# A causal segment's feature map with one exponential for all keys and one for all queries, in a four-layer attention kernel on one core

## The chip, the core and the metric

The kernel runs on one core of one Trainium2 chip. The metric is the device time of one execution in microseconds (us), lower is better. The core has five engines that run their own instruction queues and wait for each other by semaphores: PE (matrix products), ACT (exponentials and other functions), DVE (elementwise work, reads PSUM), POOL (elementwise work in SBUF) and SP (issues transfers).

## The reference

Four layers stand one behind the other on 2048 tokens of width 512, with 32 heads of 16 columns: causal segments with a memory (A), full attention (B), A, B. Cut to what matters:

```python
def _A_ref(x, wq, wk, wv, wo, beta):          # N = 4 segments of L = 512 tokens
    phi = lambda t: jnp.where(t > 0, t + 1.0, jnp.exp(t))
    for s in range(N):
        qs, ks, vs = (q[:, :, s].copy(), k[:, :, s].copy(), v[:, :, s].copy())
        p = _softmax(jnp.einsum('bhqd,bhkd->bhqk', qs, ks) * scale + mask, axis=-1)
        a_dot = jnp.einsum('bhqk,bhkd->bhqd', p, vs)
        pq = phi(qs)
        num = jnp.einsum('bhld,bhde->bhle', pq, M)
        den = jnp.einsum('bhld,bhd->bhl', pq, z)[..., None] + 1e-06
        outs.append(g * (num / den) + (1.0 - g) * a_dot)
        pk = phi(ks)
        M = M + jnp.einsum('bhld,bhle->bhde', pk, vs)
        z = z + jnp.einsum('bhld->bhd', pk)
    return joined(outs) @ wo

def _B_ref(x, wqkv, wo):                      # full attention over 2048 tokens
    p = _softmax(jnp.einsum('bhqd,bhkd->bhqk', q, k) * Dh ** (-0.5), axis=-1)
    return joined(jnp.einsum('bhqk,bhkd->bhqd', p, v)) @ wo

x = x + _A_ref(_layernorm(x), ...)            # and B, A, B in the same way
```

The feature map phi is applied to the queries of segments 1 to 3 and to the keys of segments 0 to 2, in two A layers: six times each.

## The kernel before

**Units.** Scores are made in banks: one PSUM bank holds 128 keys of one head against 512 queries. The main loop (attention, one turn is a *unit*) takes two or three banks; PE multiplies masked queries (qm) with keys, ACT takes one exponential over the unit's banks (L1925, ps to pT, 1024 or 1536 columns), and two units later PE multiplies values by pT. Two sets of three banks alternate, so PE can be at most two units ahead of ACT. Other banks of scores do not go to ACT: a unit of two banks leaves room for one or two *taken* banks, whose exponentials DVE makes with integer arithmetic in bf16 bits (L1394, ps to a tile of sixteen-bit integers) and two sums of it with constants (L1450 and L1493 on DVE, L1475 on POOL). PE multiplies values by the three parts. The integer tile is dxt, or KA, QA, VA, wA or wB while those are free. So a bank costs either ACT a third of a unit or DVE, POOL and PE some work each. On the causal diagonal the mask is a product with tri on PE, or a select on pT by POOL (L1939) where PE is late.

**Tasks between units.** Layer norms, projections (xT with wA or wB, evacuated from PSUM by DVE, or by ACT in a copy at L757), the memory and the output projection are generators (task_A, task_mem, task_B, task_out). Each yields its needs with its cost on PE and DVE; the loop resumes one when its needs are met and it fits.

**The order.** Every instruction is recorded ahead of time by a planner (Sched) that keeps an estimated time of each engine; the program that runs is the fixed order per engine that comes out. How eager each kind of work is (how late DVE may be, how many banks are taken, when PE is kept busy with products on zeros, who does a mask) is set by some 60 limits, chosen for every stretch of 20 units in the table PLAN; a limit that a row leaves out has its default. A new limit or a new cost anywhere changes all that is planned behind it.

**The feature map.** task_A calls phi four times per segment: for keys, after four transposes through the DMA (phk from KA), in two halves of 1024 columns; for queries in two halves from QA to phq. Each half has an exponential on ACT into the tile amem (L966), then on DVE max(x, 0) + 1 (L968) and the minimum with the exponential (L969). amem also carries the memory's output (task_mem, L1059) through a transpose into phq, so a half waits until amem is free. The memory's output is later added to oT by DVE (L1211) or POOL (L1186, L1208). The masked queries qm of the next group are made on POOL as well (L1802).

Of the kernel before, what the change touches and what calls it, by code (L numbers as in the profile page):

```python
# [6 lines left out]
ACT = mybir.ActivationFunctionType  # L7
ALU = mybir.AluOpType
# [408 lines left out]
class Builder:  # L417
# [3 lines left out]
        0: dict(TAKEN_A=1, FILL_DVE=400, MASK_PE=800, PE_LOW=7, GAP=3, QMIN=3, OPART=0, DIV_LATE=2500, PACE=2, DX_LATE=1700, HURRY=1500, POOL_QM=1, POOL_C=0, CR_A=1200, CR_LOW=2000),  # L421
        1: dict(ACT1=300, MARGIN=600, R_LATE=2200, NEAR=5, CR_W=1300, CR_B=1800, R_PAIRS=2, DIV_LATE=2500, TAKEN=0.5, DVE_LATE=800, BG_BANK=100, PHI_LATE=300, OPART=3, NEARW=20, POOL_C=0, DX_LAG=1, POOL_D=2500, REST=8, EARLY=500, POOL_QM=1, DX_FIN=3000, DMA_LATE=1200, TRADE=400, FILL_DVE=400, ORD=13, PACE=12, DMA_STEPS=2, HOLD_AT=12, PE_B=2, TAKEN_A=1, MASK_PE=800, PE_LOW=7, PE_A=4, POOL_MEM=0),
        2: dict(FILL_DVE=400, MASK_PE=800, GAP=3, BG_BANK=400, QMIN=3, LOW=20, POOL_QM=1, ACT1=600, R_PAIRS=2, PE_LOW=7, DX_LATE=1700, DX_FIN=3000, OPART=3, HOLD_AT=12, PE_A=4, NEAR_A=50, TRADE=0, TAKEN_A=1, PART=3, DMA_LATE=700, CR_B=1200, SLACK=350, DMA_STEPS=0, POOL_WAIT=600, MARGIN=250, EVAC_ACT=1500),
        3: dict(R_LATE=1200, NEARW=40, PAIRS=999, MASK_PE=800, LEVEL=3, TAKEN=0.5, LOW=20, MARGIN=600, TAKEN_A=1, EARLY=300, OPART=3, QUAD=0, FILL=0.47, CR_A=1200, DX_LATE=700, CARRY_W=1500, PART=3, CR_W=2200, HOLD_MAX=0, DVE_LATE=1700, FILL_DVE=400, BUSY_WAIT=500, ACT1=300, QMIN=3, PE_LOW=7, PE_A=6, TRADE=400, DVE_LATE_LOW=2500, PACE=7, PE_B=6, ORD=3, POOL_WAIT=600),
        4: dict(R_LATE=1200, NEARW=40, PAIRS=999, MASK_PE=800, LEVEL=3, TAKEN=0.5, LOW=20, MARGIN=600, TAKEN_A=1, EARLY=300, OPART=0, QUAD=0, FILL=0.47, DX_BANK=900, CR_A=1200, DX_LATE=700, CARRY_W=1500, PART=3, CR_W=2200, HOLD_MAX=0, DVE_LATE=1700, FILL_DVE=400, BUSY_WAIT=500, ACT1=300, QMIN=3, PE_LOW=7, PE_A=6, TRADE=0, DVE_LATE_LOW=2500, POOL_D=2500, PACE=7, PE_B=6, POOL_MEM=0),
        5: dict(ACT1=300, NEAR=8, TAKEN_A=1, PV_SKIP=900, FILL_DVE=400, BACK=8, CR_W=2200, NEARW=40, OPART=0, TAKEN=0.4, LOW=20, DVE_LATE=800, QWAIT=8, HOLD_AT=40, PHI_LATE=0, REST=20, POOL_D=2500, R_LATE=1200, MARGIN=350, EARLY=300, QUAD=0, CR_A=1700, CARRY_W=1500, PART=3, BUSY_WAIT=500, PE_LOW=7, PE_A=6, HURRY=4000, PAIRS=999, LEVEL=3, DX_BANK=900, DX_LATE=700, QMIN=3, TRADE=0, DVE_LATE_LOW=2500, PACE=7, DVE_FIN=1500, MASK_PE=800, FILL=0.47),
        6: dict(ACT1=300, NEAR=8, TAKEN_A=1, PV_SKIP=900, FILL_DVE=400, BACK=8, CR_W=2200, NEARW=40, OPART=0, TAKEN=0.4, LOW=20, DVE_LATE=800, QWAIT=8, HOLD_AT=40, PHI_LATE=0, REST=20, POOL_D=2500, R_LATE=1200, MARGIN=350, EARLY=300, QUAD=0, CR_A=1700, CARRY_W=1500, PART=3, BUSY_WAIT=500, PE_LOW=7, PE_A=6, HURRY=4000, PAIRS=999, LEVEL=3, DX_BANK=900, DX_LATE=700, QMIN=3, TRADE=400, DVE_LATE_LOW=2500, PACE=7, DVE_FIN=1500, MASK_PE=800, FILL=0.47, DMA_LATE=0),
        7: dict(R_LATE=1200, NEARW=40, PAIRS=999, MASK_PE=800, LEVEL=3, TAKEN=0.4, LOW=20, MARGIN=350, TAKEN_A=1, EARLY=300, OPART=0, QUAD=0, FILL=0.47, DX_BANK=900, CR_A=1200, DX_LATE=700, CARRY_W=400, PART=3, CR_W=2200, HOLD_MAX=0, DVE_LATE=800, FILL_DVE=400, BUSY_WAIT=500, ACT1=300, DMA_LATE=0, GAP=3, QWAIT=8, NEAR=8, PE_A=6, POOL_QM=1, DVE_LATE_LOW=2500, PACE=7, DVE_FIN=200, HURRY=1500, PV_SKIP=900, POOL_D=2500, PE_LOW=7, QMIN=3),
        8: dict(R_LATE=1200, NEARW=40, PAIRS=999, MASK_PE=800, LEVEL=3, TAKEN=0.4, LOW=30, MARGIN=500, TAKEN_A=1, EARLY=500, OPART=0, QUAD=0, FILL=0.47, DX_BANK=900, CR_A=1200, DX_LATE=700, CARRY_W=1500, PART=3, CR_W=2200, DVE_LATE=1700, FILL_DVE=400, BUSY_WAIT=500, ACT1=300, DMA_LATE=0, QWAIT=8, NEAR=8, PV_SKIP=900, NEAR_A=0, HURRY=1500, QMIN=3),
        9: dict(MARGIN=600, NEAR=3, PV_SKIP=200, FILL_DVE=100, BUSY_ROOM=900, FILL=0.4, CR_W=1500, CARRY_W=400, R_PAIRS=2, OPART=4, GAP=3, DVE_LATE=800, QMIN=1, HOLD_AT=40, POOL_QM=1, ACT1=300, DX_LATE=900, REST=8, CR_B=1800, DX_LAG=1, BACK=6, LOW=14, BUSY_WAIT=500, POOL_D=1200, PART=3, PHI_LATE=0, EVAC_ACT=100, RUSH0=40, AHEAD=1000, RUSH=120, DX_TAIL=300, FIT=3),  # L430
# [68 lines left out]
    MASK_PE = 500  # L499
    MASK_POOL = 2000  # L500
    PHI_LATE = 100
    POOL_MEM = 1500
# [3 lines left out]
    NEARW = 60  # L506
# [6 lines left out]
    PORT_FREE = 0  # L513
# [448 lines left out]
    def phi(self, src, bsrc, dst, bdst):  # L962

        et = self.amem[:, :, :, :].rearrange("p a b c -> p a (b c)")
        yield [("free", self.b_amem, bsrc)], 0, 0
        self.op("act", lambda e: e.activation(et, src, ACT.Exp), reads=bsrc, writes=self.b_amem, ns=1023, gap=915)  # L966
        yield [("at", self.step + 2)], 0, 1130
        self.op("dve", lambda e: e.tensor_scalar(dst, src, 0.0, 1.0, op0=ALU.max, op1=ALU.add), reads=bsrc, writes=bdst, ns=430)  # L968
        self.op("dve", lambda e: e.tensor_tensor(dst, dst, et, ALU.min), reads=self.b_amem + bdst, writes=bdst, ns=729)  # L969
# [1396 lines left out]
```

## Time and profile before

| | |
|---|---|
| median of 3 runs | 1660.99 us (1660.08 to 1661.16) |
| the profiled execution | 1660.92 us, its span 1659.2 us |
| busy, share of the span | ACT 98%, PE 95%, DVE 84%, POOL 74% |
| units (L1925) | 1503: 1050 of two banks, 453 of three |
| the feature map's exponentials (L966) | 24, of 1024 columns |

The span runs from the first to the last instruction. A matrix product's end is modelled and products overlap, so PE's 95% is not a full PE; an engine's busy time and what it waits for are read together.

### The profile page before, as it was taken

What the parts mean: (1) busy time and instruction counts of PE and PEld (TensorE: products, weight loads), DVE (VectorE), ACT (ScalarE), POOL (GpSimd) and SP (SyncE); (2) the same over time, 40 slices, a digit from 0 to 9 for tenths busy, and PEclk for the clock granted to TensorE, in tenths of its full rate; (3) what the DMA queues carried; (4) which work ended last, traced back from release to release, by engine and by line L of the source; (5) the groups of instructions that cost most, each with busy time, mean ns of one, the idle gap of its engine ahead of it and who ended that gap; (6) DMA issues with size and microseconds to landing.
All of it is one profiled execution on the core that took longest, in us unless ns stands there. A gap on an engine that the chain in (4) does not pass through costs nothing.

```text
span 1659.2 us, 45418 instructions
## 1 busy us (share of the span) xinstructions
PE 1573.7 (95%) x19667; PEld 568.6 (34%) x19738; DVE 1397.2 (84%) x2232; ACT 1622.0 (98%) x1575; POOL 1227.6 (74%) x1322
## 2 busy tenths in 40 slices
PE   8999999999999999999999999999999999999998
PEld 5553435222222535222235222442222222222236
DVE  5668666979998687899878997779899999999996
ACT  7999999999999999999999999999999999999998
POOL 3342234779898443699875898577899999999995
PEclk9999999999999999999999999999999999999999
DMA  6211211001120322200212102112001200100000
GB/s 185 41 21 26 40 27 28 8 8 30 23 62 11 72 68 43 58 11 14 58 24 31 49 14 55 18 21 53 1 14 24 46 11 11 27 11 11 22 16 19
DMA packets 148424, 54.46 MB, mean 33 GB/s; under 512 B 128768, under 2 KB 147712, under 8 KB 148224
## 3 DMA queue, kind: packets, MB, share of 16 engines
q1 hardware_dynamic: 148224, 51.56, 14.8%
q8 instruction: 154, 2.52, 0.7%
q14 instruction: 46, 0.38, 0.1%
HBM read 18.88 MB, written 2.10 MB: 13 GB/s over the span
## 4 chain that ended last, share of the span: by engine, by line
ACT 60%; PE 25%; DVE 9%; DMA 2%; POOL 2%; issue 1%; SPq 0%; ACTq 0%; POOLq 0%
ACT pT L1925 59%; PE ps L683 24%; DVE KA L1394 2%; DVE dxt L1394 1%; ACT amem L966 1%; DVE wA L1394 1%; DVE wB L1394 1%; DMA tb<-ub 1%; DMA xT<-xn 1%; DMA phq<-amem 1%; DMA phk<-KA 0%; SPq L766 0%; POOL pT L1939 0%; DVE lnst L873 0%; DVE xn L895 0%
## 5 line engine op out<-in xcount | busy, mean ns | idle before, releaser
L1925 ACT ACTIVATE pT<-ps 128x1024 bf16<-128x1024 f32 (+1 forms) x1503 | 1592.0, 1230 | 21.0 <-PE ps L683 18.1
L683 PE MATMUL ps<-qm,KB 32*128 32x512 bf16 x4096 | 543.9, 385 | 53.3 <-ACT pT L1925 39.0
L683 PE MATMUL ps<-pT,VB 128*17 128x512 bf16 x2751 | 476.7, 384 | 1.6 <-DVE dxt L1394 0.7
L1475 POOL TENSOR_TENSOR dxt<-dxt,shift 128x512 int32<-128x512 int32 (+1 forms) x293 | 312.8, 1079 | 103.2 <-DVE dxt L1394 73.3
L1394 DVE TENSOR_SCALAR KA<-ps 128x512 uint16<-128x512 f32 (+1 forms) x438 | 339.3, 793 | 24.1 <-PE ps L683 21.7
L683 PEld LDWEIGHTS ps<-qm,KB 32*128 32x128 bf16 x4096 | 139.4, 91 | 558.7 <-ACT pT L1925 442.5
L1394 DVE TENSOR_SCALAR dxt<-ps 128x512 uint16<-128x512 f32 (+1 forms) x332 | 257.3, 789 | 27.3 <-PE ps L683 25.7
L1475 POOL TENSOR_TENSOR QA<-KA,shift 128x512 int32<-128x512 int32 x208 | 227.3, 1103 | 53.4 <-DVE KA L1394 52.9
L683 PE MATMUL ps<-dxt,VB 128*17 128x512 bf16 x1125 | 249.8, 381 | 0.3 <-POOL dxt L1475 0.3
L683 PEld LDWEIGHTS ps<-pT,VB 128*17 128x17 bf16 x2751 | 111.0, 87 | 272.8 <-issue 257.4
L1475 POOL TENSOR_TENSOR VA<-KA,shift 128x512 int32<-128x512 int32 x172 | 184.7, 1083 | 24.0 <-DVE QA L1450 18.5
L1939 POOL TENSOR_SCALAR_AFFINE_SELECT pT<-pT 128x512 bf16<-128x512 bf16 (+4 forms) x135 | 71.7, 546 | 170.7 <-ACT pT L1925 170.4
L1475 POOL TENSOR_TENSOR wA<-wA,shift 128x512 int32<-128x512 int32 (+1 forms) x140 | 151.8, 1096 | 9.8 <-DVE wA L1394 6.4
L683 PE MATMUL ps<-QA,VB 128*17 128x512 bf16 x499 | 145.6, 381 | 0.0
L683 PE MATMUL ps<-VA,VB 128*17 128x512 bf16 x499 | 143.6, 381 | 0.0
L1475 POOL TENSOR_TENSOR wB<-wB,shift 128x512 int32<-128x512 int32 x114 | 124.0, 1102 | 5.9 <-DVE wB L1394 4.3
L683 PE MATMUL ps<-KA,VB 128*17 128x512 bf16 x499 | 127.6, 381 | 0.0
L1394 DVE TENSOR_SCALAR wA<-ps 128x512 uint16<-128x512 f32 (+1 forms) x150 | 120.6, 817 | 8.2 <-PE ps L683 7.3
L683 PE MATMUL ps<-wA,VB 128*17 128x512 bf16 x558 | 125.4, 381 | 0.0
L1394 DVE TENSOR_SCALAR wB<-ps 128x512 uint16<-128x512 f32 (+1 forms) x128 | 103.7, 823 | 4.9 <-PE ps L683 4.7
L683 PE MATMUL ps<-VA,pT 128*128 128x51 bf16 (+1 forms) x2488 | 103.0, 187 | 1.4 <-POOL pT L1939 0.6
L683 PE MATMUL ps<-wB,VB 128*17 128x512 bf16 x471 | 104.2, 381 | 0.0
(174 smaller groups left out, 2061.6 us busy)
## 6 DMA issues: line engine op xcount, KB each, us to landing
wB<-in_B_wqkv_dram SPq DMA_DIRECT2D x48, 128.0 KB, 2.4
wA<-in_A_wk_dram SPq DMA_DIRECT2D x16, 128.0 KB, 2.4
wA<-in_A_wq_dram SPq DMA_DIRECT2D x16, 128.0 KB, 2.6
wA<-in_A_wv_dram SPq DMA_DIRECT2D x16, 128.0 KB, 2.8
out_dram<-x SPq DMA_DIRECT2D x8, 256.0 KB, 2.2
x<-in_A_x_dram SPq DMA_DIRECT2D x3, 512.0 KB, 9.7
wB<-in_B_wqkv_dram SPq DMA_DIRECT2D x1, 1536.0 KB, 12.8
oT<-ob SPq DMA_TRANSPOSE x63, 2.5
```

Source lines behind the costliest of these rows:

```text
L683: self.sc.add("pe", lambda e: e.matmul(out, lhsT, rhs, start=start, stop=stop, skip_group_check=True), reads=reads, banks=[(bank, "w", all ...
L966: self.op("act", lambda e: e.activation(et, src, ACT.Exp), reads=bsrc, writes=self.b_amem, ns=1023, gap=915)
L1394: self.op("dve", lambda e: e.tensor_scalar(d, o, SCALE * LOG2E * 128, 127.0 * 128 + EXP_BIAS, op0=ALU.mult, op1=ALU.add), writes=self.b_dx ...
L1475: self.op("pool", lambda e: e.tensor_tensor(d, s, c, ALU.add), reads=src + [self.b_shift] + [first] * k, writes=dst, ns=165 + 1.75 * n, ga ...
L1925: self.sc.add("act", (lambda dst, src: lambda e: e.activation(dst, src, ACT.Exp, scale=SCALE))(dst, src), writes=self.b_pT[slot * 3 + i:sl ...
L1939: self.op("pool", (lambda blk, pat: lambda e: e.affine_select(blk, blk, pattern=pat, compare_op=ALU.is_ge, fill=0.0, base=0, channel_multi ...
```

## The change

phi takes all four chunks at once: one exponential of 2048 columns, and behind it two pairs of DVE operations, each on half. For keys the exponential goes to xT, the transposed input of the projections, which the segment has used up by then, and no longer waits for amem; for queries it goes straight to phq, and max(x, 0) + 1 goes to amem. The cost given to the planner is one exponential of 1880 ns (1770 from one to the next) instead of 1023 (915). In PLAN 53 of the 76 rows are new: many are copies of a neighbouring row, or a row with a few limits changed. The core of the diff:

```diff
 class Builder:
     PLAN = {
...
-        3: dict(R_LATE=1200, NEARW=40, PAIRS=999, MASK_PE=800, LEVEL=3, TAKEN=0.5, ..., OPART=3, ..., FILL_DVE=400, ..., PE_B=6, ORD=3, POOL_WAIT=600),
+        3: dict(R_LATE=1200, NEARW=40, PAIRS=999, MASK_PE=800, LEVEL=3, TAKEN=0.5, ..., OPART=0, ..., DX_BANK=900, ..., FILL_DVE=100, ..., POOL_D=2500, PACE=7, PE_B=6, POOL_MEM=0),
...
-    def phi(self, src, bsrc, dst, bdst):
-
-        et = self.amem[:, :, :, :].rearrange("p a b c -> p a (b c)")
-        yield [("free", self.b_amem, bsrc)], 0, 0
-        self.op("act", lambda e: e.activation(et, src, ACT.Exp), reads=bsrc, writes=self.b_amem, ns=1023, gap=915)
+    def phi(self, src, bsrc, dst, bdst, et=None, bet=None):
+
+        own = et is None
+        et, bet = (dst, bdst) if own else (et, bet)
+        amem = self.amem[:, :, :, :].rearrange("p a b c -> p a (b c)")
+        yield [("free", bet, bsrc)], 0, 0
+        self.op("act", lambda e: e.activation(et, src, ACT.Exp), reads=bsrc, writes=bet, ns=1880, gap=1770)
         yield [("at", self.step + 2)], 0, 1130
-        self.op("dve", lambda e: e.tensor_scalar(dst, src, 0.0, 1.0, op0=ALU.max, op1=ALU.add), reads=bsrc, writes=bdst, ns=430)
-        self.op("dve", lambda e: e.tensor_tensor(dst, dst, et, ALU.min), reads=self.b_amem + bdst, writes=bdst, ns=729)
+        for i in (0, 2):
+            if i:
+                yield [], 0, 1130
+            s, d, t = src[:, i:i + 2, :], dst[:, i:i + 2, :], et[:, i:i + 2, :]
+            bs, bd = bsrc[i:i + 2] if own else bsrc, bdst[i:i + 2]
+            o, bo = (amem, self.b_amem) if own else (d, bd)
+            self.op("dve", (lambda o, s: lambda e: e.tensor_scalar(o, s, 0.0, 1.0, op0=ALU.max, op1=ALU.add))(o, s), reads=bs, writes=bo, ns=430)
+            self.op("dve", (lambda d, o, t: lambda e: e.tensor_tensor(d, o, t, ALU.min))(d, o, t), reads=bo + (bd if own else bet), writes=bd, ns=729)
...
-            for j in range(2):
-                yield [("dma", ("phk", L, s))] + read, 0, 0
-                a, ba = self.phk[:, 2 * j:2 * j + 2, :], self.b_phk[2 * j:2 * j + 2]
-                yield from self.phi(a, self.b_phkc + ba, a, ba)
+            yield [("dma", ("phk", L, s))], 0, 0
+            a = self.phk[:, :, :]
+            yield from self.phi(a, self.b_phkc + self.b_phk, a, self.b_phk, self.xT[:, slot, :, :], self.b_xT[slot])
             self.flags.add(("phk", L, s))
         self.give_xT(slot)
         if s > 0:
-            for c in (0, 2):
-                yield [("op", L, s - 1), ("mem", L, s - 1)] + ([("dma", ("amemT", L, s - 1, 3))] if s > 1 else []), 0, 0
-                yield from self.phi(self.QA[:, sl, c:c + 2, :], self.b_QA[sl][c:c + 2], self.phq[:, c:c + 2, :], self.b_phq[c:c + 2])
+            yield [("op", L, s - 1), ("mem", L, s - 1)] + ([("dma", ("amemT", L, s - 1, 3))] if s > 1 else []), 0, 0
+            yield from self.phi(self.QA[:, sl, :, :], self.b_QA[sl], self.phq[:, :, :], self.b_phq)
             self.flags.add(("phq", L, s))
```

The order moves everywhere. Three places follow, before and then after; lines below the change are numbered 5 higher in the new kernel.

ACT in the second segment of the first layer (units 40 to 51). Before:

```order
L1925 ACTIVATE pT<-ps 128x1536 x2
L966 ACTIVATE amem<-phk 128x1024
L1925 ACTIVATE pT<-ps 128x1536 x3
L966 ACTIVATE amem<-phk 128x1024
L1925 ACTIVATE pT<-ps 128x1536 x3
L966 ACTIVATE amem<-QA 128x1024
L1925 ACTIVATE pT<-ps 128x1536 x3
L966 ACTIVATE amem<-QA 128x1024
L1925 ACTIVATE pT<-ps 128x1536 x14
```

After:

```order
L885 ACTIVATE lnw<-lnw 128x4
L1930 ACTIVATE pT<-ps 128x1536 x6
L968 ACTIVATE xT<-phk 128x2048
L1930 ACTIVATE pT<-ps 128x1536 x5
L968 ACTIVATE phq<-QA 128x2048
L1930 ACTIVATE pT<-ps 128x1536 x15
```

Four exponentials between units have become two of double width, three units later for the keys.

DVE at a segment of the third layer, where keys and queries follow each other (ps to QB, VB are the next layer's evacuations, rd and ob a finished group). Before:

```order
L968 TENSOR_SCALAR phk<-phk 128x1024
L969 TENSOR_TENSOR phk<-phk,amem 128x1024
L759 CAST VB<-ps 128x32x16 x2
L968 TENSOR_SCALAR phk<-phk 128x1024
L969 TENSOR_TENSOR phk<-phk,amem 128x1024
L2037 RECIPROCAL rd<-ps 128x16
L2043 TENSOR_TENSOR ob<-ps,rd 128x16x16
L759 CAST VB<-ps 128x32x16
L968 TENSOR_SCALAR phq<-QA 128x1024
L969 TENSOR_TENSOR phq<-phq,amem 128x1024
```

After:

```order
L976 TENSOR_SCALAR phk<-phk 128x1024
L977 TENSOR_TENSOR phk<-phk,xT 128x1024
L976 TENSOR_SCALAR phk<-phk 128x1024
L977 TENSOR_TENSOR phk<-phk,xT 128x1024
L759 CAST VB<-ps 128x32x16
L2042 RECIPROCAL rd<-ps 128x16
L2048 TENSOR_TENSOR ob<-ps,rd 128x16x16
L976 TENSOR_SCALAR amem<-QA 128x1024
L977 TENSOR_TENSOR phq<-amem,phq 128x1024
L976 TENSOR_SCALAR amem<-QA 128x1024
L977 TENSOR_TENSOR phq<-amem,phq 128x1024
```

The two halves of the keys, and those of the queries, now stand next to each other, where evacuations of PSUM stood between them.

POOL at the border of the first to the second layer (oT is the attention's output, to which the memory's output in phq is added; qm from QB are the second layer's first masked queries). Before:

```order
L1802 TENSOR_SCALAR qm<-QA,par 128x512 x2
L1939 AFFINE_SELECT pT<-pT 128x3x128
L1126 MEMSET VB 128x32 x2
L1186 TENSOR_SCALAR oT<-oT,gfm 128x512
L1208 TENSOR_TENSOR oT<-oT,phq 128x512
L1186 TENSOR_SCALAR oT<-oT,gfm 128x512
L1208 TENSOR_TENSOR oT<-oT,phq 128x512
L1802 TENSOR_SCALAR qm<-QB,par 128x512 x2
L1186 TENSOR_SCALAR oT<-oT,gfm 128x512
```

After:

```order
L1807 TENSOR_SCALAR qm<-QA,par 128x512 x2
L1191 TENSOR_SCALAR oT<-oT,gfm 128x512
L1213 TENSOR_TENSOR oT<-oT,phq 128x512
L1191 TENSOR_SCALAR oT<-oT,gfm 128x512
L1213 TENSOR_TENSOR oT<-oT,phq 128x512
L1131 MEMSET VB 128x32
L1807 TENSOR_SCALAR qm<-QB,par 128x512 x2
L1131 MEMSET VB 128x32
L1191 TENSOR_SCALAR oT<-oT,gfm 128x512
```

Two sums with a transferred operand stand ahead of qm in both; a memset moved behind them.

109 lines of the change are left out of this document (54 added, 55 removed).

## The prediction

> **What bounds the kernel now.** The page comes first: span, busy shares, the chain that ended last.
>
> ```profile
> span 1659.2 us, 45418 instructions
> ...
> PE 1573.7 (95%) x19667; PEld 568.6 (34%) x19738; DVE 1397.2 (84%) x2232; ACT 1622.0 (98%) x1575; POOL 1227.6 (74%) x1322
> ...
> ACT 60%; PE 25%; DVE 9%; DMA 2%; POOL 2%; issue 1%; SPq 0%; ACTq 0%; POOLq 0%
> ```
>
> ACT is busy for 1622.0 of 1659.2 us: whatever is added to ACT's work is added to the time, unless ACT's 37.2 us of idle time shrink. So two numbers are needed, ACT's work after the change and what can still be taken from that idle time. The busy times by stretch say where it lies (columns PE, DVE, ACT, POOL busy with counts, PE's clock), and the waits of ACT say for whom.
>
> ```profile
> core 0: us, PE busy (x) PEld busy (x) DVE busy (x) ACT busy (x) POOL busy (x), PEclk, DMA share, GB/s
> 0.00:20.00 20.00, 15.11 (x193) 10.23 (x195) 11.70 (x32) 10.35 (x15) 5.41 (x21) 1.00 0.89 297
> 20.00:100.00 80.00, 75.67 (x1194) 43.72 (x1209) 50.94 (x116) 76.11 (x65) 29.75 (x51) 1.00 0.26 51
> 100.00:300.00 200.00, 187.57 (x2583) 83.64 (x2596) 138.08 (x267) 195.76 (x166) 77.74 (x111) 0.99 0.15 26
> 300.00:1160.00 860.00, 820.19 (x10143) 286.46 (x10172) 732.01 (x1182) 848.77 (x827) 646.05 (x693) 1.00 0.17 35
> 1160.00:1640.00 480.00, 460.22 (x5254) 134.46 (x5253) 456.71 (x623) 478.29 (x493) 463.60 (x445) 1.00 0.08 17
> 1640.00:1660.00 20.00, 14.96 (x318) 10.12 (x318) 7.72 (x15) 12.72 (x14) 5.03 (x4) 0.95 0.08 28
> ```
> ```profile
> ACT pT L1925 <- PE ps L683: 16.4, 39, 1.4
> ...
> ACT pT L1925 <- PE ps L683: 1.2, 5, 0.3
> ```
>
> ACT's idle time is 9.65 us in the first 20 us (loads, the first layer norm), 3.89, 4.24 and 11.23 us in the next three stretches, 1.71 us in 1160 to 1640, and the rest in the tail. The first row of waits is for 20 to 1160 us, the second for 1160 to 1640: in the middle ACT waits 16.4 us for PE's scores, in the last third 1.2 us. Start and tail are the same code in both kernels; what can be won is some 18 us, nearly all of it before 1160 us.
>
> **The change on ACT.** A unit's cost is the spacing of back-to-back exponentials, not the duration of one, since they overlap.
>
> ```profile
> 99.14 1.45 ACT L1925 ACTIVATE pT<-ps 128x1536 bf16<-128x1536 f32 x1
> 157.96 4.13 ACT L1925 ACTIVATE pT<-ps 128x1536 bf16<-128x1536 f32 x3
> 163.66 10.01 ACT L1925 ACTIVATE pT<-ps 128x1024 bf16<-128x1024 f32 x8
> 173.45 1.17 ACT L966 ACTIVATE amem<-phk 128x1024 bf16<-128x1024 bf16 x1
> 174.40 1.56 ACT L1925 ACTIVATE pT<-ps 128x1536 bf16<-128x1536 f32 x1
> 281.23 1.94 ACT L1925 ACTIVATE pT<-ps 128x1024 bf16<-128x1024 f32 x2 [1.39 <-PE ps L683]
> 283.49 1.02 ACT L1925 ACTIVATE pT<-ps 128x1024 bf16<-128x1024 f32 x1 [0.32 <-PE ps L683]
> 285.75 1.45 ACT L1925 ACTIVATE pT<-ps 128x1536 bf16<-128x1536 f32 x1 [1.24 <-PE ps L683]
> ```
> ```profile
> L1925 ACT ACTIVATE pT<-ps 128x1024 bf16<-128x1024 f32 x1050 | 1004.6, 1110 | 9.6 <-PE ps L683 7.8
> L1925 ACT ACTIVATE pT<-ps 128x1536 bf16<-128x1536 f32 x453 | 649.1, 1508 | 11.4 <-PE ps L683 10.3
> ```
>
> Two of two banks take 1.94, one 1.02: spacing 0.92. Three of three banks take 4.13, one 1.45: (4.13 - 1.45)/2 = 1.34. A bank more in a unit costs 0.42 us, and a 512-wide copy spaces at 0.92 - 0.42 = 0.50. The feature map's exponential: the units ahead of it end at 173.67, the unit behind it at 175.96, so it takes 175.96 - 173.67 - 1.34 = 0.95.
> - Exponentials: 24 of 1024 columns become 12 of 2048. No row has 2048; 0.95 + 2 x 0.42 = 1.79 against 1.90 for two, so 12 x 0.11 = -1.3 us. Ends: 0 (2048 costs two of 1024) and 12 x (1.90 - 1.76) = -1.7 (1.34 + 0.42).
> - Units: the built programs have 1503 units each, but with 464 of three banks for 453 and 1039 of two for 1050: 11 banks more stay on ACT, 11 x 0.42 = +4.6 us.
> - Evacuations: 11 copies of 512 on ACT for 7: 4 x 0.50 = +2.0 us.
>
> ACT's work grows by 5.3 us, although the change takes twelve exponentials away. By place: from unit 1000 on (1159 us in this trace: the four rows up to 1160 count 1073 ACT instructions, 72 of the 1575 are no units; up to there the two programs have taken 3098 and 3097 banks of scores) 74 units have three banks for 64, and one more copy runs: +4.7 us. Ahead of it there is one such unit more, three copies, and the saving: +0.6 us.
>
> **The other engines.** DVE evacuates 11 banks of scores fewer; its feature-map operations keep number and shape (12 pairs each on keys and queries). POOL gets 3 more sums of 512 columns, 9 more of 256 and 20 more masks. PE's flipped value products go from 6402 to 6362, its mask products from 385 to 347. None of these engines ends the chain by itself; their work counts only where ACT waits for PE:
> - 20 to 100 us. In units 20 to 59 PE has 10 full-width projection products fewer (they moved to other units), 4 masks of 256 and 7 of 128 fewer, 12 more products on taken banks, 16 more of the memory's denominators, and 11 more that only keep it busy.
>
> ```profile
> L683 PE MATMUL ps<-tri,ident 128*128 128x256 bf16 x235 | 46.2, 278 | 0.0
> L683 PE MATMUL ps<-xT,wA 128*128 128x512 bf16 x101 | 28.4, 379 | 2.7 <-POOL pT L1939 0.8 <-issue 0.5 <-DVE QA L759 0.2
> L683 PE MATMUL ps<-tri,ident 128*128 128x128 bf16 x150 | 21.8, 223 | 0.0
> L683 PE MATMUL ps<-VA,dxt 128*128 128x51 bf16 x132 | 5.2, 187 | 0.0
> L683 PE MATMUL ps<-Mz,phq 128*128 128x8 bf16 x96 | 3.5, 167 | 0.0
> ```
>
>   By busy time over count: 10 x 0.28 + 4 x 0.20 + 7 x 0.15 = 4.6 us less, 16 x 0.04 + 12 x 0.04 = 1.1 us more: PE is 3.5 us shorter where ACT idles 3.9. I take -2.5; ends 0 (the waits are for order, not for work) and -3.5.
> - The wait at 281 us. POOL adds memory parts to oT; the second operand's transfer is late, the masked query (qm) of the next layer stands behind it on POOL, PE waits for qm, ACT for PE.
>
> ```profile
> 276.74 1.16 POOL L1208 TENSOR_TENSOR oT<-oT,phq 128x512 bf16<-128x512 bf16 x1 [3.69 <-DMA phq<-amem]
> ...
> 279.84 1.36 POOL L1802 TENSOR_SCALAR qm<-QB,par 128x512 bf16<-128x512 bf16 x2
> ```
> ```profile
> 280.59 0.39 PE L683 MATMUL ps<-qm,KB 32*128 32x512 bf16 x1 [1.39 <-POOL qm L1802]
> ```
> ```profile
> 281.00:285.00 4.00, 3.52 (x58) 2.28 (x58) 3.80 (x6) 2.96 (x3) 2.69 (x4) 0.70 0.19 40
> 285.00:289.00 4.00, 3.99 (x55) 1.61 (x54) 1.70 (x4) 3.25 (x3) 3.33 (x6) 0.88 0.00 0
> ```
>
>   ACT loses 1.39 there, and 0.32 + 1.24 right behind, where PE's clock is granted at 0.70 and 0.88: 2.95 us. After the change qm still stands behind two of these sums (the order of POOL); whether the transfer is late again no order tells. Half of it, -1.5; ends 0 and -3.0. [...]
>
> **The sum.** The profiled execution took 1660.92 us (span 1659.2), 0.07 under the median of 1660.99. 1660.92 + 5.3 - 2.5 - 1.5 = 1662.2 us, +0.08%. Faster or slower is told by 0.2%, 3.3 us; this is no change.
>
> **The rivals.**
> *Slower: DVE's feature map in one piece.* The two halves now share one exponential, and in 7 of the 12 places DVE runs maximum, minimum, maximum, minimum in a row; before, other work stood between the halves at all twelve.
>
> ```profile
> L969 DVE TENSOR_TENSOR phk<-phk,amem 128x1024 bf16<-128x1024 bf16 x12 | 8.9, 739 | 0.4
> L968 DVE TENSOR_SCALAR phk<-phk 128x1024 bf16<-128x1024 bf16 x12 | 6.3, 522 | 0.0
> ```
>
>   0.52 + 0.74 = 1.26 us for a half on keys. What stands behind in DVE's queue (reciprocals that free the sums' bank, copies that free the projections' bank, and through them PE) is held 1.26 us longer at those places. ACT holds at most two units ahead (1.8 to 2.7 us by the spacings), so it decides if PE's lead is below some 1.3 us when the block begins; in the stretches of the feature maps PE is late often enough (16.4 us in 39 waits). Up to 7 x 1.26 = 8.8 us; with two thirds of it, 1662.2 + 5.8 = 1668.0. For it: those waits. Against: a half of 1.26 us cost ACT 0.3 us in all before (the wait for phk, below).
>
> ```profile
> ACT amem L966 <- DVE phk L969: 0.3, 1, 0.3
> ```
> ```profile
> L969 DVE TENSOR_TENSOR phk<-phk,amem x12: 691/693/1060, 47.0 to 882.3; 128x1024 bf16<-128x1024 bf16 x12
> ```
>
>   [...]
> *Slower too: the waits stay.* If neither -2.5 nor -1.5 comes, the time is 1666.2.
> *Faster: the limits take more of the middle's waits.* 16.4 us of waiting for PE stand there, 4.0 of which I have used. PE's 512-wide keep-busy products go from 257 to 304, a sign that PE runs ahead of ACT more often. To be faster by 0.2% it must give 8.6 us in all; with 12, 1660.9 + 5.3 - 12 = 1654.2. Against: the last third has 1.7 us to give and gets 4.7 more work, with DVE at 456.71 and POOL at 463.60 of 480 us, so all must come from before 1160 us.
> *The merge does nothing.* If a 2048-wide exponential costs as much as two, 1663.5: the same verdict.
>
> **How the numbers follow.** No change (1662.2, or 1663.5): 0.40; its own range is 1657.7 to 1664.2. Slower (block on DVE 0.14, waits that stay 0.16): 0.30, 1664.3 to 1670. Faster: 0.30, 1652 to 1657.6. The range leaves a tenth out on either side: 1653.5 to 1668.5, that is ACT's +5.3 with 12.7 us less idle time, or with 2.3 us more. The work on ACT is counted and certain to about 1 us; the idle time is what I can't read from an order.
>
> **What would show it.** Right: ACT's spacing across a 2048-wide exponential near 1.79; ACT's busy time some 5 us up, to about 1627; from the thousandth unit to the end some 3 to 5 us longer than here; less idle time on ACT in 20 to 100 us, about 1.5; in the same layer border no wait for qm, or the same. The block on DVE shows as waits of PE or ACT for banks within 3 us of the four operations. Wrong: if ACT's busy time falls, the spacing isn't its cost; if idle time before 1160 us falls below 10 us, the limits did more than the order let me see.

## The result and the profile after

The changed kernel takes 1676.95 us (median of 3 runs, 1676.71 to 1679.51) against 1660.99; the ratio is 1.0102, 95% interval 1.0079 to 1.0125. It is slower by 16 us. The forecast was 1662.2 with a range from 1653.5 to 1668.5. The profiled execution has a span of 1675.0 us against 1659.2. Lines of the new kernel are numbered 5 higher.

The page of the new kernel: span, busy shares, the chain that ended last.

```profile
span 1675.0 us, 45620 instructions
...
PE 1581.0 (94%) x19759; PEld 567.0 (34%) x19834; DVE 1395.5 (83%) x2198; ACT 1629.8 (97%) x1567; POOL 1241.9 (74%) x1352
...
ACT 64%; PE 27%; DVE 5%; DMA 1%; issue 1%; POOL 1%; SPq 1%; another core or an unknown queue 0%; ACTq 0%; DVEq 0%; POOLq 0%
```

The span grew by 15.8 us: ACT's busy time by 7.8 (1622.0 to 1629.8), its idle time by 8.0 (37.2 to 45.2). The same stretches as before (columns PE, PEld, DVE, ACT, POOL busy with counts, PE's clock, share of DMA, GB/s) and ACT's waits for PE, first from 20 to 1160 us, then from 1160 to 1640:

```profile
0.00:20.00 20.00, 15.39 (x197) 10.35 (x199) 11.66 (x33) 10.78 (x16) 4.42 (x19) 1.00 0.87 295
20.00:100.00 80.00, 74.95 (x1217) 43.65 (x1233) 54.75 (x119) 75.24 (x63) 31.33 (x57) 1.00 0.32 50
100.00:300.00 200.00, 185.99 (x2604) 83.26 (x2619) 135.70 (x265) 192.61 (x161) 75.87 (x114) 1.00 0.14 27
300.00:1160.00 860.00, 819.16 (x10122) 284.02 (x10152) 724.13 (x1157) 847.87 (x817) 657.43 (x710) 1.00 0.17 35
1160.00:1640.00 480.00, 454.94 (x4926) 124.14 (x4924) 449.43 (x595) 475.99 (x486) 450.29 (x432) 1.00 0.09 18
```
```profile
ACT pT L1930 <- PE ps L683: 20.4, 42, 1.8
...
ACT pT L1930 <- PE ps L683: 3.3, 6, 1.2
```

ACT's idle time rose in every stretch but the first: 3.89 to 4.76, 4.24 to 7.39, 11.23 to 12.13, 1.71 to 4.01 us. ACT's instructions by form, and its timeline at the wide exponential and the layer border where ACT had lost 2.95 us before:

```profile
L1930 ACT ACTIVATE pT<-ps 128x1024 bf16<-128x1024 f32 x1039 | 997.7, 1112 | 8.0 <-PE ps L683 5.5
L1930 ACT ACTIVATE pT<-ps 128x1536 bf16<-128x1536 f32 x464 | 666.0, 1510 | 21.0 <-PE ps L683 19.7
L968 ACT ACTIVATE phq<-QA 128x2048 bf16<-128x2048 bf16 x6 | 11.6, 1935 | 0.0
L968 ACT ACTIVATE xT<-phk 128x2048 bf16<-128x2048 bf16 x6 | 11.5, 1910 | 1.0 <-DMA phk<-KA 1.0
```
```profile
261.25 4.18 ACT L1930 ACTIVATE pT<-ps 128x1536 bf16<-128x1536 f32 x3
265.24 1.98 ACT L968 ACTIVATE phq<-QA 128x2048 bf16<-128x2048 bf16 x1
267.04 3.78 ACT L1930 ACTIVATE pT<-ps 128x1024 bf16<-128x1024 f32 x3
271.12 19.91 ACT L1930 ACTIVATE pT<-ps 128x1536 bf16<-128x1536 f32 x16 [0.30 <-PE ps L683]
```

The units end at 265.43, the wide exponential at 267.22: it takes 1.79 us, as forecast. The wait for qm at the layer border did not come back: ACT waits 0.30 us for PE there, and then 16 units pass from 271.12 with no wait inside. So these small sizes were right and the total was not.

### The profile page after: what moved, and what is told of

Its sections match the earlier page's. It is cut to its first block, busy times and chain, and to the rows that moved or that the text cites. A ratio compares the mean times of both kernels' runs of the same rounds, so it can differ in the third digit from the quotient of the medians.

```text
span 1675.0 us, 45620 instructions
## 1 busy us (share of the span) xinstructions
PE 1581.0 (94%) x19759; PEld 567.0 (34%) x19834; DVE 1395.5 (83%) x2198; ACT 1629.8 (97%) x1567; POOL 1241.9 (74%) x1352
## 4 chain that ended last, share of the span: by engine, by line
ACT 64%; PE 27%; DVE 5%; DMA 1%; issue 1%; POOL 1%; SPq 1%; another core or an unknown queue 0%; ACTq 0%; DVEq 0%; POOLq 0%
ACT pT L1930 63%; PE ps L683 26%; SPq L766 1%; DMA phk<-KA 1%; DVE KA L1399 0%; DVE wB L1399 0%; DVE dxt L1399 0%; ACT xT L968 0%; ACT phq L968 0%; DVE xn L895 0%; DMA phq<-amem 0%; DVE VB L759 0%; DVE qm L1807 0%; DVE wA L1399 0%; PE ps L710 0%
## 5 line engine op out<-in xcount | busy, mean ns | idle before, releaser
L1930 ACT ACTIVATE pT<-ps 128x1024 bf16<-128x1024 f32 (+1 forms) x1503 | 1598.2, 1235 | 28.9 <-PE ps L683 25.2
L1480 POOL TENSOR_TENSOR dxt<-dxt,shift 128x512 int32<-128x512 int32 (+1 forms) x316 | 333.6, 1065 | 117.4 <-DVE dxt L1399 109.7
L1399 DVE TENSOR_SCALAR KA<-ps 128x512 uint16<-128x512 f32 (+1 forms) x361 | 286.4, 810 | 32.0 <-PE ps L683 30.2
L1480 POOL TENSOR_TENSOR QA<-KA,shift 128x512 int32<-128x512 int32 (+1 forms) x188 | 206.6, 1108 | 45.1 <-DVE KA L1399 44.7
L1944 POOL TENSOR_SCALAR_AFFINE_SELECT pT<-pT 128x256 bf16<-128x256 bf16 (+4 forms) x155 | 81.8, 541 | 175.2 <-ACT pT L1930 174.6
L1480 POOL TENSOR_TENSOR VA<-KA,shift 128x512 int32<-128x512 int32 x151 | 163.4, 1089 | 6.3 <-DVE QA L1455 0.4
L1399 DVE TENSOR_SCALAR wA<-ps 128x512 uint16<-128x512 f32 (+1 forms) x182 | 143.0, 804 | 9.3 <-PE ps L683 8.8
L1480 POOL TENSOR_TENSOR wB<-wB,shift 128x512 int32<-128x512 int32 (+1 forms) x125 | 134.4, 1087 | 8.7 <-DVE wB L1399 6.3
L683 PE MATMUL ps<-VA,VB 128*17 128x512 bf16 x417 | 120.0, 381 | 0.3 <-POOL VA L1480 0.3
L683 PE MATMUL ps<-QA,VB 128*17 128x512 bf16 x417 | 116.0, 381 | 0.0
L683 PE MATMUL ps<-qm,KA 32*128 32x128 bf16 (+2 forms) x1536 | 95.3, 254 | 11.7 <-ACT pT L1930 6.4
```

What stands on the lines that cost most here:

```text
L683: self.sc.add("pe", lambda e: e.matmul(out, lhsT, rhs, start=start, stop=stop, skip_group_check=True), reads=reads, banks=[(bank, "w", all ...
L1399: self.op("dve", lambda e: e.tensor_scalar(d, o, SCALE * LOG2E * 128, 127.0 * 128 + EXP_BIAS, op0=ALU.mult, op1=ALU.add), writes=self.b_dx ...
L1480: self.op("pool", lambda e: e.tensor_tensor(d, s, c, ALU.add), reads=src + [self.b_shift] + [first] * k, writes=dst, ns=165 + 1.75 * n, ga ...
L1930: self.sc.add("act", (lambda dst, src: lambda e: e.activation(dst, src, ACT.Exp, scale=SCALE))(dst, src), writes=self.b_pT[slot * 3 + i:sl ...
L1944: self.op("pool", (lambda blk, pat: lambda e: e.affine_select(blk, blk, pattern=pat, compare_op=ALU.is_ge, fill=0.0, base=0, channel_multi ...
```

## The experiments

Any new cost or limit makes the planner write a new order, so most of these kernels keep an order as it was planned and change single instructions in it: the planner runs as before, every recorded operation is kept with the tiles that it reads and writes, the edit is made, and the waits are derived anew from those tiles (replay in the diffs; its argument names the operations that go).

### The map alone in an order that stays

In the order before, with the dependencies anew:

```diff
-        # two exponentials of 1024, each behind its own units
+        a0.fn = lambda e: e.activation(et, src, ACT.Exp)      # all four chunks, at the first one's place
+        rec[id(a0)][1:3] = [bsrc, bet]                        # keys: phk -> xT, queries: QA -> phq
+        gone[id(a1)] = a0                                     # the second one goes
```

> The order of every engine is the one before, instruction for instruction; only the feature map differs: at the place of the first of each two exponentials stands the one of 2048 columns, the second is gone from ACT (12 instructions fewer), keys go to xT and queries to phq as in the change, and the four DVE operations stay where they stood. Theory A (the loss is in the new order that the new limits make, the merge itself is sound): before 1661.0 less 12 times about 0.11 us, 1659.7 us, between 1658.5 and 1661. Theory B (the double exponential itself holds up PE or ACT, since 1.8 us of ACT stand in one piece): most of the measured 16 us is here too, 1668 or more. Theory C (four DVE operations in a row): as theory A, since here they stand apart.

Measured: 1666.45 us (1665.44 to 1668.12), 1.0034 of before (1.0022 to 1.0047). Theory A falls: with 1.3 us less work on ACT and nothing else moved the kernel is 5.5 us slower. Theory B's 1668 is not reached either: a third of the 16 us is here, not most of it. Outside the map's places the two traces agree unit by unit, to within 1 us in all, so what happens there can be read off. ACT in the second segment, first in the kernel before:

```profile
80.60 1.05 ACT L966 ACTIVATE amem<-phk 128x1024 bf16<-128x1024 bf16 x1
81.55 4.12 ACT L1925 ACTIVATE pT<-ps 128x1536 bf16<-128x1536 f32 x3
85.54 1.08 ACT L966 ACTIVATE amem<-phk 128x1024 bf16<-128x1024 bf16 x1
86.49 4.15 ACT L1925 ACTIVATE pT<-ps 128x1536 bf16<-128x1536 f32 x3
```

then with the merged map in the same order (the lines of the units are numbered 54 higher), and there the waits of PE for ACT from 80 to 101 us (in all, times, longest); before, the second row read 0.3 us in that stretch:

```profile
81.43 1.90 ACT L2378 ACTIVATE xT<-phk 128x2048 bf16<-128x2048 bf16 x1
83.23 5.48 ACT L1979 ACTIVATE pT<-ps 128x1536 bf16<-128x1536 f32 x4
89.14 2.79 ACT L1979 ACTIVATE pT<-ps 128x1536 bf16<-128x1536 f32 x2 [0.42 <-PE ps L735]
```
```profile
PEld ps L735 <- ACT pT L1979: 2.5, 3, 1.2
PE ps L735 <- ACT pT L1979: 1.9, 2, 1.1
```

The doubled exponential makes PE wait 1.1 us for a bank. ACT wins back the time of the second half four units later, but finds PE late and waits 0.42 us. Over the whole kernel ACT's waits for PE rise from 18.1 to 22.6 us; by the spacing of its instructions ACT loses 6.6 us more than before, all but less than 1 us of it within a few units of the map's places.

> As the merged map in the old order, with one thing more: the second two DVE operations of each feature map are moved up directly behind the first two, at all 12 places, so that 2.0 us of DVE stand in one piece as they do at 7 places of the new kernel. Theory A: each block can make PE wait for DVE once for up to 1 us, and part of it is caught up; 1659 to 1663 us. Theory C (the block is what costs): 12 places with the price taken before the run for 7 (5.8 us) give 10 us, 1670 us.

```diff
+            self.tuck(t1, m0)      # maximum, minimum of the second half directly behind the first half's
+            self.tuck(m1, t1)
```

Measured: 1670.06 us (1667.36 to 1671.96), 1.0050 (1.0036 to 1.0064), 3.6 us more than with the pairs apart. The block on DVE costs 0.3 us a place, a third of what the rival in the forecast took. That the time meets theory C's 1670 is luck: C counted 10 us for the block alone, and 5.5 of them are the merge's.

> The new kernel's order, instruction for instruction; only each exponential of 2048 columns is two of 1024, one directly behind the other at its place. Theory A: 12 times about 0.11 us more than the new kernel, 1678.2 us (1677 to 1680): the double width is worth its 1.3 us and nothing else. Theory B: if one long instruction is what holds the units up, nothing changes or a little is won back by the first half's earlier end, 1674 to 1677 us.

```diff
-        self.op("act", lambda e: e.activation(et, src, ACT.Exp), ...)
+        self.op("act", lambda e: [e.activation(et[:, i:i + 2, :], src[:, i:i + 2, :], ACT.Exp) for i in (0, 2)][1], ...)
```

> The new kernel unchanged, beside the others on the same chip, so that differences of 1 us can be read: 1676.95 us as first measured, within 1 us, under every theory.

Measured on the same chip: split 1677.62 us (1676.43 to 1680.85), 1.0103 (1.0090 to 1.0117); the new kernel again 1679.35 us (1676.47 to 1681.41), 1.0109 (1.0096 to 1.0123). The new kernel came 2.4 us above its first median, outside the 1 us expected. No difference can be told between the two: the scatter of 4 to 5 us from run to run in both hides 1.3 us, and with it the choice between the two theories.

> The merged map in the old order, with each exponential of 2048 columns as two of 1024, one directly behind the other at the same place. Theory B, now as: ACT is taken for 1.8 us in one piece while PE may be only two units ahead, PE stands still and has no slack to win it back. Then two adjacent halves cost what one wide instruction cost, and 1.3 us of ACT more: 1666.5 + 1.3 = 1667.8 us (1666.5 to 1669). Rival E (it is the single wide instruction, not the time in one piece): back to before and 1 us more, 1661 to 1663.

> The old order with both halves at their old places, 3 units apart as before; only the tiles are those of the change (keys to xT, queries to phq, the maximum to amem). Theory B: the time before, 1661.0 us (1660 to 1662.3). Rival D (the loss comes from the tiles and the waits that they bring, not from where ACT's work stands): 1666 us, as the merged map in the old order.

```diff
 # halves_adjacent: the merged map in the old order, but
+                a0.fn = lambda e: [e.activation(et[:, i:i + 2, :], src[:, i:i + 2, :], ACT.Exp) for i in (0, 2)][1]
 # halves_new_tiles: both halves where they were, into the new tiles
+            for i, a in ((0, a0), (2, a1)):
+                a.fn = lambda e: e.activation(et[:, i:i + 2, :], src[:, i:i + 2, :], ACT.Exp)
```

Measured: adjacent 1668.28 us (1666.27 to 1668.68), 1.0044 (1.0032 to 1.0057); new tiles 1660.43 us (1658.39 to 1661.15), 0.9999 (0.9990 to 1.0008). Rivals D and E fall. The tiles cost nothing and the wide instruction is not the fault; what costs is where on ACT the second half's time stands.

> The kernel before in its own order, with the second exponential of each feature map left out (its two DVE operations take the first half's values instead), so ACT has 12 instructions of 0.94 us less and nothing stands elsewhere. If ACT alone sets the pace at these places: 12 times 0.94 is 11.3 us less, 1649 us. Theory F (at these places PE has as little to spare as ACT, so time taken from ACT comes back as waiting for PE; the merged map in the old order lost 0.5 to 0.9 us a few units behind most places in that way): 1654 to 1658.5, likeliest 1656.

```diff
+        self.sc.replay({id(p[0]): q[0] for q, p in zip(self.phis[::2], self.phis[1::2])})   # every second exponential goes
```

Measured: 1660.38 us (1658.68 to 1661.74), 0.9997 (0.9988 to 1.0006). Taking 11.3 us of work by its spacing (1622.0 to 1613.1 us of busy time) from the engine that is busy for 98% of the span gains nothing that can be told, less even than theory F's 1654 to 1658.5. The same place in this kernel, and the busy times ahead of its wait (columns as above):

```profile
80.95 1.05 ACT L1018 ACTIVATE amem<-phk 128x1024 bf16<-128x1024 bf16 x1
81.89 5.49 ACT L1979 ACTIVATE pT<-ps 128x1536 bf16<-128x1536 f32 x4
87.81 2.79 ACT L1979 ACTIVATE pT<-ps 128x1536 bf16<-128x1536 f32 x2 [0.43 <-PE ps L735]
```
```profile
85.00:87.81 2.81, 2.81 (x45) 1.73 (x45) 2.14 (x5) 2.38 (x3) 2.81 (x5) 1.00 0.00 0
```

A unit behind the second half's old place ACT now waits 0.43 us for PE, and PE is busy for all of the 2.81 us up to the end of that wait. Unit by unit, at eleven of the twelve places at most half of the 0.94 us is left four units later; at the tenth all of it is left, until ACT waits 1.3 us for DVE at the eleventh. Over the whole kernel ACT's waits for PE rise from 18.1 to 25.5 us, and those for DVE at the map from 0.3 to 1.6. So at most of the map's places PE has no time to spare either, and the second half mostly lay in time that ACT would have waited anyway. Made earlier, it no longer covers that wait, and it holds PE up as well.

> The merged map in the old order, but its exponential of 2048 columns stands at the place of the second half instead of the first, and the first half's two DVE operations move behind the second half's, so that the four stand in a row. To be compared with the merged map with the block at the early place, 1670.1 us. Theory B (1.8 us in one piece with PE two units ahead): the same piece, 1669 to 1671. Theory F (what costs is that ACT is 0.9 us late for 3 units where the order of the others has no slack): ACT is early instead, the ACT part of the loss (5.4 us) mostly goes and the DVE block's stays, 1664 to 1667.

```diff
+            a1.fn = lambda e: e.activation(et, src, ACT.Exp)   # the wide one at the second half's place
+            gone[id(a0)] = a1
+            self.tuck(t0, m1)                                   # the first half's pair behind the second's
+            self.tuck(m0, t0)
```

Measured: 1674.78 us (1673.59 to 1677.41), 1.0088 (1.0075 to 1.0102), slower than either forecast, and 4.7 us slower than at the early place. ACT being early does not help (theory F in that form falls): ACT only waits for PE sooner (31.8 us in all against 26.4), and the wide piece holds PE up where it then stands. Why this place costs 4.7 us more stays open. The minima come later, and with them the memory's products on PE, which was not tried apart; and PE's mean clock was 0.994 to 0.997 in these runs against 0.997 to 1.000 at the early place.

> The opposite of the change, in the old order and with the new tiles: each exponential of 1024 columns becomes two of 512, the first one unit's exponential earlier on ACT where its inputs are planned to be there, so that no piece of the map takes ACT for more than about 0.5 us. ACT has 24 instructions more, each with about 0.07 us of its own, +1.7 us. Theory B: PE's stalls shrink by something between nothing and half of the 6.6 us that the doubling added, so 1659.4 to 1662.7, likeliest 1661. Rival D or a theory in which pieces do not matter: 1662.7 or more.

> The new kernel's order, with each exponential of 2048 columns as two of 1024, the second at its place and the first 1 to 3 units' exponentials earlier on ACT where its inputs are planned to be there, which is so at 9 of 12 places; the other 3 stay together. Theory B: the new kernel's 1678 us (1676.95 and 1679.35 so far), plus 1.3 us of ACT, less 9 twelfths of 6.6 us, 1674 us (1672 to 1676). Theory A (all the loss is in the rest of the new order): 1678 + 1.3, 1679 us.

```diff
+                new = self.put(mark, piece(et, src, 2 * j), ...)      # an exponential's first part, up to 1 (quarters)
+                a.fn = piece(et, src, 2 * j + 1)                      # or 3 (new order) units' exponentials earlier
```

Quarters: 1666.07 us (1664.58 to 1670.36), 1.0038 (1.0026 to 1.0051), above theory B's range and within what the rival allows (1662.7 or more). Unbunched: 1684.89 us (1683.00 to 1687.72), 1.0148 (1.0134 to 1.0162), above both theories. The first row is the quarters on keys with their idle time ahead (behind the bar), the second a wait of the unbunched halves:

```profile
L2396 ACT ACTIVATE xT<-phk 128x512 bf16<-128x512 bf16 x24 | 15.3, 638 | 2.5 <-DVE phk L2420 2.3
```
```profile
ACT xT L2399 <- DMA phk<-KA: 3.4, 4, 1.3
```

Moved ahead, pieces waited for DVE (2.3 us) and for the transposes of the keys (3.4 us), and ACT with all its units behind them. That explains part; at the queries these exponentials did not wait, and the times show no gain from them either. So smaller pieces, placed like this, are not the cure in either order; whether a place without these waits would do better was not tried.

### The limits

> The change's feature map with the limits of before; the planner makes the order anew. If limits and map are fitted to each other to the single order (theory A): ACT has 8.6 us more work by the count of its instructions, and waits that nobody has fitted come on top, 1685 to 1750 us. Rival (the map carries the loss, the limits repair part of it or nothing): 1661 to 1680.

> The old feature map in halves with the limits of the change; the planner makes the order anew. Theory A: as far off as the map alone, since these limits were chosen for another map; 18.1 us more work on ACT by the count of its instructions and unfitted waits, 1695 to 1760 us. Rival (the new limits as such are better or equal, the map is what costs): 1655 to 1670.

The edits are the two halves of the change: phi and task_A of one kernel with the table PLAN of the other. One run each: 1754.72 us and 1775.21 us, 94 and 115 us slower than before and somewhat above theory A's ranges. So neither half of the change can be read by itself: in both runs limits that were chosen for another map give an order that is far worse than the 16 us in question.

> The new kernel's order with the feature map cut down to max(x, 0) + 1: the 12 exponentials of 2048 columns (21.6 us of ACT) and the 24 minima (16.6 us of DVE) are left out, nothing else moves. Theory H (the map has no part in the loss, which is made by the order that the new limits give, above all behind unit 940): 1671 to 1678 us, still 10 us or more above the kernel before. Theory B (the wide exponential holds up the new order as it did the old one): the map's share of the loss goes, 1666 or less. If ACT paced everywhere: 1678 less 21.6, 1656.

> The same cut in the order before: 24 exponentials of 1024 columns (22.6 us of ACT) and 24 minima left out. After the half map's 1660.4 us, theory H: 1657 to 1661. If ACT paced everywhere: 1638.

```diff
+            for a in exps:
+                gone[id(a)] = (the operation of ACT ahead of it)
+            for t, m, s, d, bd in pairs:
+                t.fn = lambda e: e.tensor_scalar(d, s, 0.0, 1.0, op0=ALU.max, op1=ALU.add)
+                gone[id(m)] = t
```

Measured: new order 1669.75 us (1665.80 to 1671.80), 1.0054 (1.0041 to 1.0067); old order 1655.78 us (1654.30 to 1658.36), 0.9975 (0.9965 to 0.9985). Both lie below theory H's ranges, by 1.3 and 1.2 us, and neither reaches the times for an ACT that paces everywhere. The pages, new order first, and the waits of ACT for PE:

```profile
PE 1582.0 (95%) x19759; PEld 568.1 (34%) x19834; DVE 1378.8 (83%) x2174; ACT 1611.7 (97%) x1555; POOL 1240.4 (74%) x1352
```
```profile
ACT pT L1983 <- PE ps L735: 37.0, 77, 1.8
```
```profile
PE 1569.9 (95%) x19667; PEld 567.5 (34%) x19738; DVE 1380.0 (83%) x2208; ACT 1603.6 (97%) x1551; POOL 1226.0 (74%) x1322
```
```profile
ACT pT L1978 <- PE ps L735: 29.6, 73, 1.1
```

With exponentials and minima of both maps left out, the new order is still 14.0 us behind the old one. These instructions can't cause that part; that the new order was laid out around them, and keeps something of their price when they are gone, is not excluded. The instructions themselves are worth 4.5 us in the old order (1660.25 - 1655.78) and 7.2 to 9.6 in the new one (1676.95 and 1679.35 - 1669.75, measured on different chips), so their part in the loss is some 3 to 5 us. In both orders the 18 us of busy time that ACT loses turn mostly into waiting for PE: 25.2 to 37.0 us and 18.1 to 29.6.

> The change's feature map with limits searched anew, stretch by stretch, by a short search that starts from the limits of before and never sees the change's own. By the count of its instructions ACT has 4.4 us more work than before (447 units of three banks and 1061 of two, 14 copies), against 5.4 in the new kernel. Theory H (the new limits are poor, the map costs about 5 us): 1665 to 1672 us, some 8 us faster than the new kernel. Rival I (with this map no order does better than the change's): 1676 or more.

> The old feature map in halves with limits found by the same search, as long, which starts from the limits of the change and never sees those of before. ACT has 0.2 us more work than before by the count. Theory H: the map's price as in the fixed old order, 5.5 us, is the difference to the merged map with searched limits, so 1660 to 1667 us. Rival J (the map costs nothing once limits are fitted to it): within 2 us of the merged map with searched limits.

The edit is the table PLAN alone, in the changed kernel and in the kernel before. Measured: merged map 1675.60 us (1674.79 to 1680.17), 1.0102 (1.0088 to 1.0116); old map 1669.01 us (1668.22 to 1669.53), 1.0056 (1.0042 to 1.0070). The absolute times missed theory H: both are higher than forecast. The merged map got no better than with the change's own limits, 0.4 us short of rival I's 1676; that no order at all does better is more than one search can show. The difference between the two is 6.6 us, near theory H's 5.5 and against rival J. And the old map, with limits searched as briefly, stands 9.5 us above the kernel before, which has the same map. So the change's limits are about as good as a short search gives; those of before are about 10 us better than that.

### One stall by itself

The largest stall behind unit 1000 in the new kernel. DVE, POOL beside it, and the stretches ahead and behind (columns as above, the clock before the last two):

```profile
1163.56 0.67 DVE L1399 TENSOR_SCALAR wA<-ps 128x512 uint16<-128x512 f32 x1
1164.16 1.19 DVE L895 TENSOR_SCALAR xn<-x,lnst,lnw 128x512 bf16<-128x512 bf16 x1
1165.27 1.87 DVE L1399 TENSOR_SCALAR wA<-ps 128x512 uint16<-128x512 f32 x3
```
```profile
1164.16 1.03 POOL L1480 TENSOR_TENSOR QA<-KA,shift 128x512 int32<-128x512 int32 x1
```
```profile
1162.00:1166.00 4.00, 3.10 (x22) 0.83 (x22) 4.00 (x6) 4.00 (x6) 3.92 (x5) 1.00 0.30 61
1166.00:1170.00 4.00, 4.00 (x19) 0.78 (x19) 1.90 (x4) 2.30 (x3) 3.84 (x5) 0.57 0.17 35
```

> The new kernel with one thing moved: the last normalization on DVE (x to xn, 1.19 us at 1164 us where others of its kind take 0.41, beside an operation of POOL) goes behind the next two exponentials of taken banks (ps to wA), for which PE waits 0.7 us and after which PE's clock was at half for 3.4 us. Theory H: the stall of 1.35 + 0.57 us and the clock's drop go, 1678 less 2 to 3 us, 1675.5. Rival (the wait is handed on to the next unit): 1677 to 1679.

```diff
+        self.tuck(self.xns[-1], q[q.index(self.xns[-1]) + 2])
```

The transposes that fetch this tile are recorded ahead of the moved operation here, so they carry the tile's earlier content; only the time is read. Measured: 1682.78 us (1679.75 to 1685.11), 1.0137 (1.0122 to 1.0153), above the ranges of theory H and of the rival. The stall itself went: the trace is within 0.1 us of the new kernel's at unit 1000 and 1.8 us ahead at unit 1002. By unit 1006 it is 0.8 us behind, and the mean clock of this profile is 0.997 where the new kernel's first has 0.999. So the wait is handed on, as the rival had it, though its time was too low. This stall could not be taken out of the order by moving this one operation.

## Why the prediction was wrong

**The step that failed first is the sentence that "whatever is added to ACT's work is added to the time, unless ACT's 37.2 us of idle time shrink".** It was read from a busy share over the whole span, and it lets the idle time only shrink; it grew by 8.0 us. At the places of the map the sentence does not hold: 11.3 us less on ACT there bought nothing, and 1.3 us less, with half of the time moved some three units ahead, cost 5.5. ACT's second exponential mostly stood in time in which ACT would have waited for PE. The trace before had a sign of it: ACT waits 16.4 us for PE in 39 waits between 20 and 1160 us. I read these waits as something to win; at the map's places they meant that PE had no slack.

**The merge, -1.3 (ends 0 and -1.7): wrong in sign.** The size of the instruction was right, 1.79 us. The price of its place was put at nothing. In the old order the merge costs +5.5, between two searched orders +6.6. No end of my range held that, and no rival named it: the slower rival put the place on DVE. That block exists (3.6 us for 12 places in the old order, so about 2 for 7, where I took 5.8) but is the smaller part.

**The waits, -2.5 and -1.5: wrong in sign, in all.** In 20 to 100 us ACT's idle time rose by 0.9 instead of falling by 2.5; PE's busy time there fell by 0.7 us (75.67 to 74.95), not by the 3.5 that I had counted from its instructions. The count gave no time to the eleven products that only keep PE busy. They come to 3.3 us (PE's busy time and count come first, before and then after):

```profile
20.00:100.00 80.00, 0.73 (x2) 0.19 (x2) 0.00 (x0) 0.00 (x0) 1.00 0.26 51
20.00:100.00 80.00, 3.99 (x13) 1.14 (x17) 0.00 (x0) 0.00 (x0) 1.00 0.32 50
```

With them the count is 0.2 us less work for PE, and next to nothing was left to win. The wait for qm at the layer border went wholly, about -2.7 where I took half; that POOL waits only 1.98 us for the transfer instead of 3.69 no step of mine had told. But ACT's idle time grew by 8.0 us over the span where I had -4.0. That is 12 of the 14.8 us by which the forecast missed.

**The work on ACT, +5.3: nearly right.** By the spacings of both traces and the counts it is +5.6: 11 x 0.426 for the units' third banks, 4 x 0.50 for the copies, less 24 x 0.944 - 12 x 1.797 = 1.1 for the map. By busy time it is +7.8. Where it lies was read too late in the program. The rows count units up to 1100 us, from 1100 to 1180 and from there on (columns PE, PEld, ACT, POOL; the count in the ACT column is that of the units), before and after:

```profile
0.00:1100.00 1100.00, 378.45 (x4129) 151.73 (x4129) 1043.57 (x941) 71.75 (x135) 1.00 0.19 39
1100.00:1180.00 80.00, 30.69 (x171) 7.16 (x169) 78.93 (x82) 0.00 (x0) 1.00 0.11 28
1180.00:1660.00 480.00, 186.22 (x1285) 51.12 (x1285) 469.54 (x482) 0.00 (x0) 1.00 0.09 18
```
```profile
0.00:1100.00 1100.00, 372.62 (x3975) 145.00 (x3975) 1038.47 (x941) 78.38 (x147) 1.00 0.19 39
1100.00:1180.00 80.00, 28.74 (x285) 10.70 (x285) 76.24 (x73) 3.39 (x8) 0.98 0.17 39
1180.00:1676.00 496.00, 189.53 (x1307) 51.79 (x1307) 483.48 (x491) 0.00 (x0) 1.00 0.08 18
```

and the first thousand units, before and after:

```profile
0.00:1158.70 1158.70, 400.66 (x4253) 156.95 (x4253) 1101.20 (x1000) 71.75 (x135) 1.00 0.19 39
0.00:1165.50 1165.50, 395.91 (x4231) 154.50 (x4231) 1101.91 (x1000) 81.78 (x155) 1.00 0.19 39
```

Both kernels have 941 units behind them at 1100 us, and the other 562 take 16 us longer in the new one. From unit 1000 to the end it takes 509.5 us where it took 500.5, 9.0 more; the forecast had 3 to 5. No instruction of the feature map stands there in either kernel, and the merged map in the old order leaves this stretch as it was (500.6 us). ACT's forms from 1100 us on, before and after:

```profile
L1925 ACT ACTIVATE pT<-ps 128x1024 bf16<-128x1024 f32 x493 | 467.4, 1136 | 1.6 <-PE ps L683 1.2
L1925 ACT ACTIVATE pT<-ps 128x1536 bf16<-128x1536 f32 x70 | 107.7, 1574 | 0.8 <-PE ps L683 0.6
```
```profile
L1930 ACT ACTIVATE pT<-ps 128x1024 bf16<-128x1024 f32 x469 | 446.7, 1138 | 2.7 <-PE ps L683 2.1
L1930 ACT ACTIVATE pT<-ps 128x1536 bf16<-128x1536 f32 x94 | 141.9, 1537 | 2.8 <-PE ps L683 2.3
```

24 more units of three banks are 10.1 us of ACT, of which I had seen the 10 units behind unit 1000. This does not put the whole loss behind 1100 us: the programs do their work in another order, and by then the new one has 13 such units fewer and more projections behind it. How the loss spreads over the stretches stays open.

**The rest of the loss, 10 to 14 us, is the order itself.** The old map with limits from a short search is 9.5 us slower than before, and with the maps cut away the new order is 14.0 us behind. Summed up as an estimate, the units and copies (+6.6) are as forecast, the merge is +5.5 for -1.3, and about +4 is left for the waits where I had -4.0. Which limits of the new table make these waits stays open. None of the other planned orders that ran is as good as the one before. The chances were wrong for the same reason: of the re-planned orders five of five are slower than before, by 9.5, 16 (twice), 94 and 115 us, and I gave slower 0.30.

Of the marks that I had named, ACT's spacing came as said and the border's wait went; ACT's busy time came to 1629.8 us where I had about 1627. The stretch from the thousandth unit on grew by twice what I had, and the idle time in 20 to 100 us and before 1160 us did the opposite of what I took.

## What to carry to other kernels

An engine that is busy for 98% of the span need not be the bound at each place; take some of its work away there, with the order held, before you price what a change adds or removes. Work on the leading engine can lie in its own waits: merging two instructions into one can move half of that work out of its cover, and here, in a fixed order with two units of slack, that cost 5.5 us where the instructions saved 1.3. And where a planner with fitted limits writes the order anew, the saving of the edit can be small beside the fit that is lost, so here slower was to be expected; separate the two by keeping the old order with the edit in it.

## What was not expected of the hardware

The runs of one kernel differ with the mean clock that PE is granted. The cut map in the new order ran in 1665.80 us at a mean clock of 1.000 and in 1671.80 at 0.996; the new kernel in 1676.47 at 1.000 and in 1681.41 at 0.997. In the new kernel's first profile the clock is granted at 0.50 in one spell of 3.41 us, from 1166.41 to 1169.82 us (0.57 over the 4.00 us in the row above), and at 1.00 ahead of it and behind it. It begins 0.41 us behind a wait of PE for DVE of 0.7 us, and PE was busy for 3.10 of the 4.00 us ahead of it. The kernel before has a spell of the same 3.41 us at 0.50 from 282.57 to 285.98 us, at the layer border. The new kernel's second profile, with the same order of instructions, has a mean clock of 0.998 where the first has 0.999. What sets the length of the spells and their places no run here shows.

A normalization on DVE took 1.19 us beside an operation of POOL (1.03 us) that began in the same moment, at 1164.16 us, where the median of its kind is 0.41; whether POOL's operation made it longer no run here shows.
